# Three matrix products into a bank that is overwritten, ahead of each of the first 22 steps of a two-layer feed-forward

## The chip, the cores and the metric

The kernel runs on one core of one Trainium2 chip. The metric is the device time of one execution in microseconds (us); lower is better. The core has a matrix engine (TensorE: PE, with PEld for its weight loads), a vector engine (VectorE: DVE), a scalar engine (ScalarE: ACT), GpSimd (POOL) and SyncE (SP), whose queue issues the transfers from memory. Each engine runs its own list of instructions in order and waits on semaphores for the others. The matrix engine's clock is throttled: the profile shows at each time what was granted, 1.0 (2.4 GHz) or 0.5 (1.2 GHz).

## The reference

Three stages follow each other. Attention with gates runs over 768 time steps, for 2 batches of 8 heads of width 40; then come a feed-forward with a sigmoid gate, and a normalised feed-forward with a SiLU gate, each over 1536 tokens of width 320 with 1536 hidden units.

```python
for t in range(S):                                   # attention, S = 768
    m_new = np.maximum(f_gate[:, :, t] + m, i_gate[:, :, t])
    f_stab = np.exp(f_gate[:, :, t] + m - m_new)
    i_stab = np.exp(i_gate[:, :, t] - m_new)
    C = f_stab[..., None, None] * C + i_stab[..., None, None] * np.einsum('bhd,bhe->bhde', vt, kt)
    n = f_stab[..., None] * n + i_stab[..., None] * kt
    h_tilde = np.einsum('bhde,bhe->bhd', C, qt)
    y[:, :, t] = o * h_tilde / np.maximum(np.abs(nq), 1.0)
...
gate = 1.0 / (1.0 + np.exp(-(x @ w_gate)))           # first feed-forward
x = gate * (x @ w_val) @ w_out
...
xn = x / rms * rms_g                                 # second feed-forward
g = xn @ w_gate
out = g * (1.0 / (1.0 + np.exp(-g))) * (xn @ w_val) @ w_out
```

## The kernel before

**Attention** is cut into 6 chunks of 128 time steps, each for both batches. A chunk is a string of small jobs (`a_f`, `a_s`, `a_p`, `a_inter`, `a_pv`, `a_u`, `a_h`, `a_x`): the matrix engine multiplies queries and keys (`a_s`, L323), VectorE weights the result (`a_p`, L332, after a scan in `a_f`, L306), the matrix engine multiplies by the values (`a_pv`, L391), VectorE adds the carried state and divides (`a_h`, L417 to L429), and `a_x` transposes the chunk (L467 to L470) into `xT`, the input of the first feed-forward, of which ScalarE writes the high half (L446 to L453) and VectorE the low one (`sub`, L194).

**The first feed-forward** is 6 chunks times 12 slices of 128 hidden units, 72 steps. A step (`moe`) is 16 products of 256 columns (L689) into a PSUM bank with the tag `g`, then a sigmoid on ScalarE (L691), a product on VectorE (L692), and a split into two halves `h` (L694 and a `sub` on GpSimd). Two steps later `moe_out` multiplies `h` by the slice of the output weights (L727, 6 products of 320 columns). There are two banks `g`, so the products of a step wait until VectorE has read the bank of the step before last.

The first 24 steps are interleaved by `ORDER = '000000111100001100111111'`, a digit for the chunk: steps 0 to 5 are slices 0 to 5 of chunk 0, steps 6 to 9 are slices 0 to 3 of chunk 1, and so on. In that stretch the weights of the layer arrive: each slice is loaded (L139), its 8-byte numbers are converted on ScalarE and VectorE (`conv_w`, L161 to L191) and split into two halves (`split_w`, L194 to L207). Attention on chunk 1 has to be done before step 6. The second feed-forward (`moe2`, L703, products of 512 columns, and L752) follows after the 72 steps, and its weights are loaded and converted over the last of them.

**The order.** The code lists jobs by step numbers (`at`, `ev`); then the framework's scheduler puts the instructions of each engine into an order, with a model of its own for their durations, and every engine keeps that order on the chip.

**Unread products** exist in the program already. `bank(tag)` hands out a PSUM bank, and if a number stands on the list `pend`, it takes it off and first issues so many products of the tile `warm` into that bank (L86, L87). The first real product overwrites them. Before, `pend` is filled twice, with 13 at the very start (L591) and with 1 later (L622). `warm` is then a zeroed tile of a pool that is closed at L675.

Of the kernel before, what the change touches and what calls it, by code (L numbers as in the profile page):

```python
# [9 lines left out]
BF16 = mybir.dt.bfloat16  # L10
# [19 lines left out]
GR = 80  # L30
SKEW = 2
WARM = 13
KEEP = (2, 14)
C2S = (8, 10)
XF = (0, 0, 0, 0, 0, 0, 0, 0, 0, 0, 0, 0)
# [29 lines left out]
def mlstm_moe_kernel(ctx, tc, gate_if, gate_s, qk, qg, tok, w1, w2, rms_g, cst, out):  # L65
# [15 lines left out]
    def bank(tag):  # L81
        if tag in cycle:
            turn[tag] += 1
            tag = cycle[tag][turn[tag] % len(cycle[tag])]
        t = (ps_2 if tag in "ag" else ps_1).tile([128, 512], F32, tag=tag, name=tag)
        for _ in range(pend.pop() if pend else 0):  # L86
            nc.tensor.matmul(out=t, lhsT=warm[:, 0:128], rhs=warm, start=True, stop=True)  # L87
        return t

    pend = []  # L90

    def keep(t, i, c, n):

        if c == 0 and i % 2 == 0:
            w = min(512 - i * n, 64 * KEEP[n == L])
            if w > 0:
# [11 lines left out]
    ident4 = const.tile([128, 4, L], F32, name="ident4")  # L108
# [84 lines left out]
    def sub(eng, out, a, b):  # L193
        eng.tensor_tensor(out=out, in0=a, in1=b, op=ALU.subtract)  # L194
# [340 lines left out]
    pos = {k: i for i, k in enumerate(seq)}  # L535
# [33 lines left out]
    for f in range(NF):  # L569
        t = pos[1, 0, f]  # L570
# [5 lines left out]
        t = W2A + int(W2B * f)  # L576
# [8 lines left out]
    warm = gp.tile([128, 512], BF16, name="warm")  # L585
# [4 lines left out]
    nc.scalar.activation(out=er[:, 0:1], in_=mhalf[0:GR], func=AF.Exp)  # L590
    pend.append(WARM)  # L591
    bank("o0")
# [81 lines left out]
    gates_r4()  # L674
    stk.close()  # L675
    hp = pool("hp", 3)
    more.append(pool("xn", 2))
    xn, xg = [], []
    load_qk(1, 0)
# [3 lines left out]
    def moe(c, f):  # L683
        x = xT[1, c]
        w = wg_t[f]
        g = bank("g").rearrange("p (m t) -> p m t", m=2)
        for m in range(2):
            for i, (ws, xs) in enumerate(ORD):
                nc.tensor.matmul(out=g[:, m, :], lhsT=w[:, m, ws, :], rhs=x[xs // 3][:, xs % 3, :], start=(i == 0), stop=(i == 7))  # L689
        sg = p2.tile([128, T], F32, tag="sig", name="sig")  # L690
        nc.scalar.activation(out=sg, in_=g[:, 0, :], func=AF.Sigmoid, scale=2.0 ** -8)  # L691
        nc.vector.tensor_tensor(out=sg, in0=sg, in1=g[:, 1, :], op=ALU.mult)  # L692
        h = hst[1, c, f] = hp.tile([128, 2, T], F32R, tag="h", name="h")
        nc.scalar.activation(out=h[:, 0, :], in_=sg, func=AF.Copy)  # L694
        sub(nc.gpsimd, h[:, 1, :], sg, h[:, 0, :])
# [73 lines left out]
    for i in range(min(ev), len(seq) + SKEW):  # L769
# [6 lines left out]
        if 0 <= i < len(seq):  # L776
            layer, c, f = seq[i]
            wo_t_used[layer, f] = wo_t[f]
            (moe if layer == 1 else moe2)(c, f)
        while 0 <= i and done < len(seq) and done <= i - (SKEW if seq[done][0] == 1 else 1):  # L780
            layer, c, f = seq[done]
# [86 lines left out]
```

## Time and profile before

| what | value |
|---|---|
| median of three runs | 525.17 us (522.12 to 525.74) |
| the profiled execution | 525.99 us, span 523.9 us |
| matrix engine busy | 492.4 us, 94% of the span |
| VectorE, ScalarE, GpSimd busy | 316.0, 249.6, 234.6 us |
| mean granted clock of the matrix engine | 0.944 |

The span is what the profile covers; 2.1 us lie around it. The shares are means over stages of different kinds: until about 113 us the weights of the first layer and the first attention chunks are prepared, from there to 250 us the matrix engine runs through the first layer, and then the weights of the second layer are made ready beside it.

### The profile page before, as it was taken

To read this page: it belongs to the slowest core of one execution; us is meant where nothing else is said; L and a number is where in the kernel's file an instruction comes from. 1 tells how busy PE (TensorE), PEld (TensorE's weight loads), DVE (VectorE), ACT (ScalarE), POOL (GpSimd) and SP (SyncE) were. 2 spreads that over 40 slices of the span, in tenths; PEclk is the share of its full clock that TensorE was granted. 3 is DMA by queue.
4 is the path that set the end of the run, shared out by engine and by line. 5 is a ranking of instruction groups with operands and counts; after the bars stand their busy time and mean duration, and the time that the engine had idled before them with its cause. 6 is when DMAs were issued, how large, how long until landed. Compare 5 with 4: busy or idle time off the path is not lost.

```text
span 523.9 us, 8522 instructions
## 1 busy us (share of the span) xinstructions
PE 492.4 (94%) x3248; PEld 450.9 (86%) x3248; DVE 316.0 (60%) x581; ACT 249.6 (48%) x535; POOL 234.6 (45%) x265
## 2 busy tenths in 40 slices
PE   6969866999999999999999888999999999999997
PEld 3859855989999999999999877788888888888886
DVE  5796898994535958758678998742343223432223
ACT  5586949762633454445558874632243222431222
POOL 1584794474253746535235997542112121122220
PEclk9575696989999999999999999999999999999999
DMA  6938545711220322202245422200000000000001
GB/s 211 317 112 294 176 145 198 244 47 35 85 74 1 81 84 74 79 2 90 77 157 210 144 94 76 76 1 1 1 35 17 0 1 0 27 24 1 1 1 50
DMA packets 13342, 43.79 MB, mean 84 GB/s; under 512 B 1846, under 2 KB 5158, under 8 KB 13302
## 3 DMA queue, kind: packets, MB, share of 16 engines
q1 hardware_dynamic: 13158, 43.12, 25.0%
q8 instruction: 25, 0.41, 0.3%
q10 hardware_dynamic: 144, 0.14, 0.1%
q14 instruction: 15, 0.12, 0.1%
HBM read 41.21 MB, written 2.01 MB: 82 GB/s over the span
## 4 chain that ended last, share of the span: by engine, by line
PE 62%; DVE 9%; ACT 6%; DMA 4%; issue 3%; POOL 2%; POOLq 0%; DVEq 0%; SPq 0%; ACTq 0%
PE g L689 13%; PE a L703 11%; PE o L752 11%; PE g L703 11%; PE o L727 7%; DMA wraw<-in_w_dram 4%; PE o L689 3%; DVE wg L194 1%; POOL wg L194 1%; DVE wc L184 1%; ACT wraw L161 1%; DVE wc L191 1%; ACT wraw L165 1%; PE a L323 1%; ACT wraw L164 1%
## 5 line engine op out<-in xcount | busy, mean ns | idle before, releaser
L689 PE MATMUL g<-xT,wg 128*128 128x256 f32 x896 | 134.1, 300 | 4.1 <-ACT wg L201 1.8
L689 PEld LDWEIGHTS g<-xT,wg 128*128 128x128 f32 x896 | 122.9, 204 | 6.2 <-DVE sig L692 2.7
L194 POOL TENSOR_TENSOR h<-sig,h 128x256 fp32r<-128x256 f32 x72 | 65.4, 911 | 91.7 <-ACT h L694 90.2
L194 POOL TENSOR_TENSOR ft<-p,fb 128x512 fp32r<-128x512 f32 x35 | 45.5, 1303 | 133.7 <-ACT fb L712 133.7
L727 PE MATMUL o<-wo,h 128*128 128x320 f32 x432 | 81.8, 320 | 7.4 <-POOL h L194 4.0
L706 DVE TENSOR_TENSOR p<-p,g 128x512 f32<-128x512 f32 x36 | 24.6, 687 | 90.1 <-ACT p L705 90.1
L727 PEld LDWEIGHTS o<-wo,h 128*128 128x128 f32 x432 | 66.8, 194 | 11.1 <-POOL h L194 6.8
L752 PE MATMUL o<-wo,fb 128*128 128x320 f32 x288 | 53.1, 311 | 0.0
L703 PE MATMUL g<-xT,wg 128*128 128x512 f32 x180 | 50.8, 394 | 0.1
L712 ACT ACTIVATE fb<-p 128x512 fp32r<-128x512 f32 (+1 forms) x37 | 22.8, 619 | 58.7 <-DVE p L711 52.4
L705 ACT ACTIVATE p<-g 128x512 f32<-128x512 f32 x36 | 21.3, 596 | 60.6 <-PE g L703 56.2
L752 PEld LDWEIGHTS o<-wo,fb 128*128 128x128 f32 x288 | 45.9, 188 | 2.4 <-ACT fb L712 0.2
L703 PE MATMUL a<-xT,wg 128*128 128x512 f32 x180 | 47.8, 390 | 0.0
L694 ACT ACTIVATE h<-sig 128x256 fp32r<-128x256 f32 x72 | 29.6, 414 | 37.2 <-DVE sig L692 35.2
L703 PEld LDWEIGHTS a<-xT,wg 128*128 128x128 f32 x180 | 33.5, 188 | 6.8
L703 PEld LDWEIGHTS g<-xT,wg 128*128 128x128 f32 x180 | 32.5, 188 | 5.6 <-ACT xT L446 0.4
L711 DVE TENSOR_TENSOR p<-p,a 128x512 f32<-128x512 f32 (+1 forms) x37 | 24.6, 672 | 21.0 <-PE a L703 20.3
L689 PE MATMUL o<-xT,wg 128*128 128x256 f32 x256 | 35.1, 285 | 0.4 <-DVE sig L692 0.4
L161 ACT ACTIVATE wraw<-wraw 128x960 f32<-128x960 f32 x24 | 26.3, 1097 | 19.3 <-DMA wraw<-in_w_dram 19.3
L692 DVE TENSOR_TENSOR sig<-sig,g 128x256 f32<-128x256 f32 x56 | 23.0, 413 | 20.1 <-ACT sig L691 18.6
L194 POOL TENSOR_TENSOR wg<-wc,wg 128x256 fp32r<-128x256 f32 (+1 forms) x34 | 27.1, 810 | 15.0 <-ACT wg L201 12.2
L689 PEld LDWEIGHTS o<-xT,wg 128*128 128x128 f32 x256 | 32.6, 191 | 0.9 <-DVE sig L692 0.9
(224 smaller groups left out, 873.1 us busy)
## 6 DMA issues: line engine op xcount, KB each, us to landing
wraw<-in_w_dram SPq DMA_DIRECT2D x24, 960.0 KB
tok<-in_tok_dram SPq DMA_DIRECT2D x12, 488.0 KB
fb<-fd SPq DMA_DIRECT2D x20, 256.0 KB
raw<-in_qk_dram SPq DMA_DIRECT2D x24, 160.0 KB
out_dram<-xn SPq DMA_DIRECT2D x12, 160.0 KB
qg<-in_qg_dram SPq DMA_DIRECT2D x10, 180.0 KB
rmsg<-in_rms_g_dram SPq DMA_DIRECT2D x1, 160.0 KB
cs<-in_cst_dram ACTq DMA_DIRECT2D x1, 136.5 KB
```

Of the source, the lines that this page charges most:

```text
L161: nc.scalar.activation(out=hi.bitcast(F32), in_=hi.bitcast(F32), func=AF.Copy, scale=2.0 ** -111)
L194: eng.tensor_tensor(out=out, in0=a, in1=b, op=ALU.subtract)
L689: nc.tensor.matmul(out=g[:, m, :], lhsT=w[:, m, ws, :], rhs=x[xs // 3][:, xs % 3, :], start=(i == 0), stop=(i == 7))
L692: nc.vector.tensor_tensor(out=sg, in0=sg, in1=g[:, 1, :], op=ALU.mult)
L694: nc.scalar.activation(out=h[:, 0, :], in_=sg, func=AF.Copy)
L703: nc.tensor.matmul(out=g[m], lhsT=w[:, m, ws, :], rhs=x[xs // 3][:, xs % 3, :], start=(i == 0), stop=(i == 7))
L705: nc.scalar.activation(out=sg, in_=g[0], func=AF.Sigmoid, scale=2.0 ** -8)
L706: nc.vector.tensor_tensor(out=sg, in0=sg, in1=g[0], op=ALU.mult)
L711: nc.vector.tensor_tensor(out=sg[:, n], in0=sg[:, n], in1=g[1][:, n], op=ALU.mult)
L712: nc.scalar.activation(out=h[0][:, n], in_=sg[:, n], func=AF.Copy)
L727: nc.tensor.matmul(out=o, lhsT=h[:, hs, n], rhs=w[:, ws, :], start=(f == 0 and i == 0), stop=(f == NF - 1 and i == 2))
L752: nc.tensor.matmul(out=o, lhsT=h[hs][:, n], rhs=w[:, ws, :], start=(f == 0 and i == 0), stop=(f == NF - 1 and i == 2))
```

## The change

`BUSY = (22, 3)`: in each of the first 22 steps of the first feed-forward, `moe` puts a 3 on `pend` before it takes its bank `g`. So three products of 512 columns go into that bank ahead of the step's 16, 66 in all. Since the zeroed tile is gone by then, `warm` becomes a view of the identity tile `ident4`, read as 16-bit numbers.

```diff
@@ -30,6 +30,7 @@
 GR = 80
 SKEW = 2
 WARM = 13
+BUSY = (22, 3)
 KEEP = (2, 14)
@@ -674,6 +675,7 @@
     gates_r4()
     stk.close()
     hp = pool("hp", 3)
+    warm = ident4.rearrange("p u t -> p (u t)").bitcast(BF16)[:, 0:512]
     more.append(pool("xn", 2))
@@ -683,6 +685,8 @@
     def moe(c, f):
         x = xT[1, c]
         w = wg_t[f]
+        if pos[1, c, f] < BUSY[0]:
+            pend.append(BUSY[1])
         g = bank("g").rearrange("p (m t) -> p m t", m=2)
```

The scheduler sees 66 more products, and orders other work differently as well. Line numbers of the changed kernel are 1 higher up to L677 and 4 higher from L689 on; its L88 is L87 of before.

**The matrix engine at steps 0 and 1.** The start of the first feed-forward, before:

```order
L400 MATMUL o_345<-vv,kk 80x84
L280 MATMUL a<-cs,gr 128x80
L689 MATMUL g<-xT,wg 128x256 x7
L280 MATMUL a<-cs,er 128x80
L689 MATMUL g<-xT,wg 128x256 x9
L283 MATMUL a<-el,selg 120x30
```

and in the change:

```order
L401 MATMUL o_345<-vv,kk 80x84
L88 LDWEIGHTS ident_80
L88 MATMUL g<-ident_80 128x512
...
L281 MATMUL a<-cs,gr 128x80
L693 MATMUL g<-xT,wg 128x256 x7
L281 MATMUL a<-cs,er 128x80
L693 MATMUL g<-xT,wg 128x256 x9
```

Six unread products, those of step 0 and of step 1, stand ahead of step 0 and of the transposes of the gates.

**The matrix engine at steps 6 to 9**, where chunk 1 enters. Before:

```order
L467 MATMUL a<-cs,x 128x128
L468 MATMUL a<-cs,x 128x128
L323 MATMUL a<-raw 128x128 x4
L470 MATMUL a<-cs,rem 128x128
L727 MATMUL o_632<-wo,h 128x320 x2
...
L689 MATMUL g<-xT,wg 128x256 x32
L369 MATMUL a<-cm,qg 128x126 x2
L369 MATMUL a<-cm,qg 128x84
L391 MATMUL a<-vv,p 128x42 x8
L689 MATMUL g<-xT,wg 128x256 x16
```

and in the change:

```order
L471 MATMUL a<-cs,rem 128x128
L324 MATMUL a<-raw 128x128 x4
L88 LDWEIGHTS ident_80
L88 MATMUL g<-ident_80 128x512
...
L693 MATMUL g<-xT,wg 128x256 x10
L324 MATMUL a<-raw 128x128 x4
L693 MATMUL g<-xT,wg 128x256 x22
L392 MATMUL a<-vv,p 128x42 x8
L88 LDWEIGHTS ident_80
L88 MATMUL g<-ident_80 128x512
...
L693 MATMUL g<-xT,wg 128x256 x16
```

The three products of step 7 stand among the transposes and output products ahead of step 6; those of step 6 stand further up, ahead of the transposes L467. From step 8 on the three stand right ahead of their step.

**VectorE, at the end of attention on chunk 1**, before (`x`, L429, is what the transposes wait for):

```order
L407 SCALAR_TENSOR_TENSOR C_106<-C_106,gb,a 120x126 x2
L407 SCALAR_TENSOR_TENSOR C_106<-C_106,gb,a 80x84
L427 SCALAR_TENSOR_TENSOR r<-hs,r 128x8
L194 TENSOR_TENSOR wg<-wc,wg 64x128
L194 TENSOR_TENSOR wo<-wc,wo 128x320
L428 RECIPROCAL r<-r 128x8
L182 TENSOR_SCALAR wc<-wraw 128x960
L429 TENSOR_TENSOR x<-x,r 128x320
```

and in the change:

```order
L195 TENSOR_TENSOR wo<-wc,wo 128x320
L429 RECIPROCAL r<-r 128x8
L430 TENSOR_TENSOR x<-x,r 128x320
L183 TENSOR_SCALAR wc<-wraw 128x960
L408 SCALAR_TENSOR_TENSOR C_106<-C_106,gb,a 120x126 x2
L408 SCALAR_TENSOR_TENSOR C_106<-C_106,gb,a 80x84
```

The update of the state (L407) and a shift of weights (L182) moved behind `x`. Further on, a scan of the next chunk (L306) moved from ahead of the low half of `xT` to behind it.

## Rows read from the trace of the kernel before

**Rows 1.** The page's slices, 40 of 13.1 us each: busy tenths, clock granted.

```profile
PE   6969866999999999999999888999999999999997
DVE  5796898994535958758678998742343223432223
PEclk9575696989999999999999999999999999999999
```

**Rows 2.** Busy time by stretch: PE, PEld, DVE, ACT, POOL; clock; DMA.

```profile
27.00:89.00 62.00, 46.45 (x249) 41.67 (x249) 52.34 (x70) 46.02 (x77) 42.52 (x49) 0.72 0.53 179
89.00:149.00 60.00, 59.28 (x442) 57.62 (x442) 44.13 (x84) 33.31 (x74) 31.75 (x43) 0.94 0.38 119
149.00:209.00 60.00, 60.00 (x538) 59.02 (x537) 38.22 (x94) 25.56 (x69) 30.96 (x40) 1.00 0.19 53
...
280.00:340.00 60.00, 54.58 (x348) 48.56 (x347) 54.10 (x81) 42.98 (x107) 47.05 (x48) 1.00 0.33 114
```

**Rows 3.** Waits of PE, 27 to 89 us: total us, times, longest.

```profile
PE a L467 <- DVE x L429: 4.2, 1, 4.2
...
PE g L689 <- ACT wg L201: 1.8, 1, 1.8
```

**Rows 4.** Waits of PE, 89 to 149 us: all there are.

```profile
PE o L727 <- POOL h L194: 0.6, 1, 0.6
PE g L689 <- DVE sig L692: 0.2, 1, 0.2
```

**Rows 5.** The chain that ended last, 108 to 122 us: start, us, what.

```profile
110.75 2.35 DVE wc L184
...
113.49 3.66 PE g L689 x16
...
118.45 1.95 PE g L689 x16
```

**Rows 6.** Timeline of PE, 57 to 95 us: start, us; idle before in brackets.

```profile
57.88 3.57 PE L689 MATMUL g<-xT,wg 128*128 128x256 f32 x15
...
77.04 0.46 PE L727 MATMUL o<-wo,h 128*128 128x320 f32 x2
81.67 0.30 PE L467 MATMUL a<-cs,x 128*128 128x128 f32 x1 [4.18 <-DVE x L429]
...
83.99 0.48 PE L470 MATMUL a<-cs,rem 128*128 128x128 f32 x1 [0.54 <-ACT rem L465]
85.25 1.43 PE L727 MATMUL o<-wo,h 128*128 128x320 f32 x4 [0.78 <-ACT h L694]
...
89.31 5.61 PE L689 MATMUL g<-xT,wg 128*128 128x256 f32 x32
```

**Rows 7.** Busy time by stretches of one clock, columns as in Rows 2.

```profile
62.30:82.70 20.40, 12.89 (x97) 11.53 (x97) 20.06 (x29) 12.85 (x22) 17.73 (x20) 1.00 0.47 168
82.80:92.90 10.10, 8.79 (x36) 7.64 (x35) 8.93 (x13) 9.09 (x21) 5.55 (x8) 0.50 0.66 196
...
113.50:116.80 3.30, 3.30 (x15) 3.30 (x16) 2.87 (x5) 2.57 (x7) 1.75 (x3) 0.50 0.33 100
```

**Rows 8.** Products of 512 columns: chain, second layer; busy time of L87 alone.

```profile
421.70 1.81 PE a L703 x8
...
4.24:5.50 1.26, 1.26 (x7) 0.49 (x5) 1.00 0.94 381
```

**Rows 9.** Timeline of DVE, 78 to 92 us.

```profile
78.01 0.80 DVE L407 SCALAR_TENSOR_TENSOR C<-C,gb,a 120x126 f32<-120x126 f32 x3
...
80.42 0.70 DVE L182 TENSOR_SCALAR wc<-wraw 128x960 int32<-128x960 int32 x1
...
86.94 1.21 DVE L306 TENSOR_TENSOR_SCAN ft<-fb,ident 128x512 f32<-128x512 f32 x1
...
89.61 1.51 DVE L194 TENSOR_TENSOR xT<-a,xT 128x256 fp32r<-128x256 f32 x5
```

**Rows 10.** The chain that ended last, 249 to 256 us: first load for layer two.

```profile
252.53 0.10 ACT sig L691
252.63 6.28 DMA wraw<-in_w_dram
```

## The prediction

> **What bounds the kernel now.** I read the slices first, to see where the matrix engine is idle and where its clock is low [rows 1]. Both lie in the first nine slices, up to about 117 us; from there to 250 us every slice is full and at full clock. So the 22 steps fall into a part with idle time and a part without, and the question is where the border runs.
>
> Busy time by stretch draws it [rows 2]. From 27 to 89 us, where steps 0 to 5 run and attention on chunk 1 ends, the matrix engine is busy for 46.45 of 62 us, so 15.5 us are idle. From 89 to 149 us, where steps 6 to 21 run, it is busy for 59.28 of 60 us, and from 149 to 209 us for all 60.
>
> The waits say what the idle time is. Before 89 us, the longest is for `x`, the last vector operation of attention on chunk 1, 4.2 us; another 1.8 us is for the weights of slice 3 [rows 3]. Between 89 and 149 us only two waits are left, 0.6 and 0.2 us [rows 4].
>
> The chain of waits needs care. Up to 113.49 us it runs over weight conversions on VectorE and ScalarE, and only then goes to the matrix engine [rows 5]. It could be read so that the matrix engine has room until 113 us. But it has been working without a pause of note since step 6 at 89.31 us [rows 6, 4]: two engines are full side by side there, and whatever is put in front of the fuller one comes out at the end.
>
> **What a product costs.** A product of 512 columns in a dense run at full clock takes 1.81 us / 8 = 0.226 us in the second layer [rows 8]. The products of `warm` at the very start are the same form as the added ones: 7 touch a stretch of 1.26 us, about 6 whole ones, 0.21 us each [rows 8]. Between 0.21 and 0.226 I take 0.226, since it comes from a full count, amid weight loads and other work as here. At half clock 15 products of 256 columns take 3.57 us [rows 6], 0.238 each, so about 0.45 for 512 columns at the most. Their weight loads ran beside the products at the start too (0.49 us of PEld in 1.26 us), and I cost them at nothing; the product before each covers them.
>
> The Trainium skill (TensorE: Matmul & The Clock Gate, Back-to-back issue gap) gives about 131 ns for a product of 512 columns in a stream of weight loads and products. By that the 42 products below would be 5.5 us, an estimate, and the sum +2.4 us; the row of 0.226 us disagrees, and I follow the row.
>
> **The change part by part.**
>
> *Steps 0 to 7: 24 products, taken at nothing.* At half clock they need 24 x 0.45 = 10.8 us, at full clock 5.4 us, against 15.5 us idle [rows 2]. Idle time has to lie in the right place, so piece by piece: the six at the front delay step 0, but ScalarE and VectorE are at weights then, and the matrix engine waits later anyway, with 1.8 us for slice 3 among it [rows 3]. Those of steps 4 to 6 fall between 62 and 82 us, where the engine is idle for 7.5 us of 20.4 while VectorE is busy for 20.06 [rows 7]. What hides them is VectorE. If that cover went, the engine would pay up to 10.8 us.
>
> *The start of steps 6 and 7: -0.7 us.* The scheduler moved three vector operations out of the way: the state update (0.80 us) and a shift (0.70 us) from ahead of `x`, and a scan (1.21 us) from ahead of the low half of `xT` [rows 9]. If all comes through, steps 6 and 7 end 2.7 us sooner. On the other side, six products at half clock (2.7 us) stand in the way of step 6, with gaps of 0.54 and 0.78 us to fall into [rows 6]; that is 1.4 us later. Between -2.7 and +1.4 I take the middle, -0.7: the vector rows say sooner, but from 85.25 us on the matrix engine worked without a pause before too, so it can't follow entirely.
>
> *Steps 8 to 21: 14 x 3 = 42 products x 0.226 = +9.5 us.* They stand directly ahead of their step, in a list that has no gaps. They use the bank `g` of that step, so where a step would wait for its bank, they wait too, and hide nothing. The real products behind them are late by 0.68 us a step; sigmoid, VectorE and GpSimd are late with them, but have time to spare there (VectorE 44.1 us busy of 60 [rows 2]).
>
> *What is given back: -0.8 us* for the two waits after 89 us [rows 4], since the vector engine no longer makes a later matrix engine wait; *and -1.6 us for the clock.* Step 12 runs at half clock from 113.5 to 116.8 us [rows 7], with 16 products in 3.66 us, against 1.95 us for step 13 at full clock [rows 5]. The pause ahead of it is one of the waits that go. I take 1.6 of the 1.7 us, with bounds of 0 and 1.7.
>
> *After step 21: nothing.* The first load of the second layer's weights starts at 252.63 us, when a sigmoid of the first layer has ended [rows 10], so it moves along with the steps. The 5.4 us idle between 280 and 340 us [rows 2] are waits for those weights, which become late by the same amount; they hide nothing.
>
> **Sum:** 9.5 - 0.8 - 1.6 - 0.7 = **+6.4 us**, so 532.4 us against the execution's own 525.99 us. That execution lies 0.8 us above the median of the runs shown and just above the highest. I take off half of that: **532.0 us**, 1.3% above the median. With the bounds of the terms (0.7 us less by the cheaper product, 2.0 us each way at step 6, 1.6 us more by the clock) the forecast's own range is 529.5 to 534.5.
>
> **The rivals.**
>
> *A. The matrix engine has room until 113 us.* Then only steps 12 to 21 pay: 30 x 0.226 = 6.8, less 0.8, 1.6 and 0.7, which is +3.7 us, or 529.3 us. For it speaks the chain, which lies on VectorE and ScalarE up to step 12 [rows 5]; against it the 59.28 us of 60 [rows 2]. It is in part true if steps 6 and 7 end sooner. Chance 0.19.
>
> *B. Nothing is given back.* The clock falls around step 6 as before and again later, and the products ahead of step 6 are paid at half speed: 9.5 - 0.8 + 1.4 = +10.1 us, or 535.7 us. For it speaks that the engine was busy for 8.79 of 10.1 us at half clock around step 6 [rows 7], so being busy alone didn't bring the clock back at once. Chance 0.14.
>
> *C. Not slower: the products keep the clock up, and the work behind them closes the gap ahead of step 6.* The place is the stretch from 77.5 us, where step 5's work ends, to 89.31 us [rows 6], the price up to 11.8 us. All of it gained would be -11.8 + 9.5 - 0.8 - 1.6 = -4.7 us, or 520.9 us; it decides from the point where step 6 starts before 82.2 us, which is 7.1 us sooner. Against it: the matrix engine waits there for VectorE, which is full and not on that clock [rows 7, 3]. Chance 0.05.
>
> The Trainium skill (TensorE: Matmul & The Clock Gate, Why this matters for your kernels) advises keeping the engine continuously busy to hold the full clock, which is the rule behind C. By it the clock would stay up around step 6; the trace has half clock there after the idle 4.2 us, which agrees, but the rule doesn't say that the faster engine ends anything sooner.
>
> *D. The products are much cheaper than the row,* near 0.13 us, as on the page above: 9.5 becomes 5.5 and the sum +2.4 us, 528.0 us. Both groups of rows for 512 columns speak against it. Chance 0.02.
>
> **How the numbers follow.** The forecast has 0.60, A 0.19, B 0.14, C 0.05, D 0.02. For 8 times in 10 I go from 528.0 to 536.0 us, which takes in the forecast, B's value and most of A, and leaves out C and the tails. One per cent of the median, about what a measurement of this kernel can tell from no change, is 5.25 us, so the border lies at 530.4 us. Three quarters of the forecast's range and B lie above it: 0.45 + 0.14 = 0.59 slower. The rest of the forecast, A and D are within: 0.15 + 0.19 + 0.02 = 0.36. C is 0.05 faster.
>
> **What would show each step right or wrong.** In the profile of the changed kernel: step 6 should start within 3 us of 89.3 us, and idle time of the matrix engine before it should have shrunk by the length of 24 products; a start before 82.2 us means C. From step 8 on, a step with its output products should take 0.68 us more than now, with no waits between 89 and 155 us; if steps 8 to 11 take more but step 12 starts where it did, A was right. The clock should be 1.0 from step 8 on; a stretch at 0.5 behind it means B. The first load of the second layer should come some 6 us later, and the rest of the trace be shifted by the same. The prediction is wrong if the order on VectorE, which the scheduler also changed, makes weights or attention late somewhere that these rows don't show, or if that later stretch takes up the delay.

## The result, and the profile after

| | before | changed |
|---|---|---|
| median (nine runs each) | 523.29 us (522.12 to 525.74) | 528.29 us (527.18 to 533.05) |
| the profiled execution | 525.99 us, span 523.9 us | 527.76 us, span 525.7 us |

The change makes the kernel slower: 1.0108 times before, 95% interval 1.0074 to 1.0143, which is 3.9 to 7.5 us; the medians differ by 5.0 us. The forecast was 532.0 us, between 528.0 and 536.0. The changed kernel's nine times lie in two groups, six from 527.2 to 528.9 us and three from 531.6 to 533.1. The two profiles come from opposite ends, that of before from above all its nine times and that of the change from its lower group, so they differ by only 1.8 us. Disturbed executions are left out of all ratios; one of the thirteen profiles, that of the kernel without products in the order of that with 24, is of one (545.1 us), and only times up to 44 us, ahead of all the steps compared here, are taken from it.

The slices of the changed kernel, of 13.1 us each, answer to [rows 1]:

```profile
PE   6969798989999999999999888999999999999997
DVE  6786999973544858659578999752343223432223
PEclk9575979999999999999999999999999999999999
```

The matrix engine is fuller in slices 6 and 7 and a little emptier in slice 9, and the clock is whole from slice 7 on, where before it dipped in slices 7 and 9. Its busy time by stretch, columns as in [rows 2]:

```profile
27.00:89.00 62.00, 52.05 (x297) 45.44 (x296) 54.34 (x76) 47.82 (x77) 47.00 (x49) 0.78 0.59 201
89.00:149.00 60.00, 57.33 (x437) 51.74 (x436) 37.01 (x69) 28.20 (x66) 29.46 (x37) 1.00 0.23 75
149.00:209.00 60.00, 60.00 (x537) 58.71 (x536) 41.34 (x97) 26.39 (x69) 32.25 (x42) 1.00 0.26 74
```

Up to 89 us it is busy 5.6 us more. From 89 to 149 us it is not fuller but emptier, 57.33 against 59.28 us, and the waits of that stretch (to 155 us; against [rows 4]) say why:

```profile
PE o L731 <- POOL h L195: 2.1, 1, 2.1
PE g L88 <- DVE sig L696: 0.5, 1, 0.5
```

The two waits that I had going away, 0.8 us, are 2.6 us now. The timeline of the matrix engine (start, us; idle before in brackets; against [rows 6]) shows where the lead came from and where that wait stands:

```profile
65.94 3.21 PE L392 MATMUL a<-vv,p 128*128 128x42 f32 x14 [2.17 <-DVE C L408]
...
77.61 0.33 PE L468 MATMUL a<-cs,x 128*128 128x128 f32 x1 [0.51 <-DVE x L430]
...
79.98 0.82 PE L88 MATMUL g<-ident 128*128 128x512 bf16 x3
...
83.80 1.35 PE L693 MATMUL g<-xT,wg 128*128 128x256 f32 x10
85.08 1.16 PE L324 MATMUL a<-raw 40*128 40x128 f32 x8
86.17 2.90 PE L693 MATMUL g<-xT,wg 128*128 128x256 f32 x22
...
92.45 2.26 PE L693 MATMUL g<-xT,wg 128*128 128x256 f32 x16
...
108.20 0.85 PE L731 MATMUL o<-wo,h 128*128 128x320 f32 x4 [2.12 <-POOL h L195]
108.89 0.82 PE L88 MATMUL g<-ident 128*128 128x512 bf16 x3
109.36 2.27 PE L693 MATMUL g<-xT,wg 128*128 128x256 f32 x16
```

The transposes of `x` start 4.06 us sooner than before, and the 4.18 us of waiting for them are 0.51. Step 6 starts at 83.80 us instead of 89.31, and its 32 products take 1.35 + 2.90 = 4.25 us instead of 5.61. Step 12 takes 2.27 us instead of 3.66. The clock of two stretches ahead of step 6 (columns as above):

```profile
66.00:72.60 6.60, 6.60 (x28) 5.76 (x29) 6.54 (x7) 2.11 (x6) 6.44 (x7) 0.50 0.49 171
73.00:83.00 10.00, 7.89 (x51) 5.86 (x49) 9.07 (x18) 9.94 (x17) 6.87 (x9) 1.00 0.34 106
```

Half clock comes earlier now, behind the 2.17 us of waiting for the state update (`C`) at 64 us, and in this profile no stretch of it is left after 73 us. Last, the chain that ended last, 108 to 122 us (start, us, what; against [rows 5]), has the price of the added products:

```profile
108.20 0.85 PE o L731 x4
109.05 0.66 PE g L88 x3
109.71 1.91 PE g L693 x16
...
113.60 0.75 PE g L88 x3
114.35 1.91 PE g L693 x16
...
117.82 0.66 PE g L88 x3
```

Three take 0.66 us, 0.22 each. Step by step the lead is used up:

| start of step | before | changed | difference |
|---|---|---|---|
| 6 | 89.31 | 83.80 | -5.5 |
| 8 | 97.13 | 92.45 | -4.7 |
| 12 | 113.49 | 109.36 | -4.1 |
| 14 | 121.12 | 118.13 | -3.0 |
| 24 | 154.53 | 156.53 | +2.0 |
| end of the span | 523.9 | 525.7 | +1.8 |

So in these two profiles the change costs 7.5 us from step 6 to step 24, and before step 6 it gains 5.5 that the forecast had as 0.7. The experiments ask which part of the change does which.

### The profile page after: what moved, and what is told of

Same layout as the page of the kernel before. It is cut to its first block, busy times and chain, and to the rows that moved or that the text cites. A ratio compares the mean times of both kernels' runs of the same rounds, so it can differ in the third digit from the quotient of the medians.

```text
span 525.7 us, 8646 instructions
## 1 busy us (share of the span) xinstructions
PE 499.8 (95%) x3314; PEld 451.3 (86%) x3314; DVE 316.2 (60%) x581; ACT 249.4 (47%) x535; POOL 241.7 (46%) x265
## 4 chain that ended last, share of the span: by engine, by line
PE 60%; DVE 11%; ACT 8%; DMA 6%; issue 3%; POOL 2%; SPq 0%; POOLq 0%
PE g L693 11%; PE o L756 11%; PE g L707 11%; PE a L707 11%; PE o L731 7%; DMA wraw<-in_w_dram 6%; PE o L693 3%; ACT wraw L162 2%; DVE wg L195 2%; PE g L88 1%; POOL wg L195 1%; PE a L324 1%; DVE wc L185 1%; DVE wc L192 1%; ACT wg L202 1%
## 5 line engine op out<-in xcount | busy, mean ns | idle before, releaser
L693 PE MATMUL g<-xT,wg 128*128 128x256 f32 x896 | 130.4, 295 | 2.9 <-DVE sig L696 1.6
L693 PEld LDWEIGHTS g<-xT,wg 128*128 128x128 f32 x896 | 118.9, 196 | 7.1 <-DVE sig L696 2.3
L195 POOL TENSOR_TENSOR h<-sig,h 128x256 fp32r<-128x256 f32 x72 | 66.5, 925 | 85.4 <-ACT h L698 84.7
L731 PE MATMUL o<-wo,h 128*128 128x320 f32 x432 | 80.2, 315 | 6.5 <-POOL h L195 5.4
L731 PEld LDWEIGHTS o<-wo,h 128*128 128x128 f32 x432 | 65.4, 190 | 9.9 <-POOL h L195 8.0
L707 PEld LDWEIGHTS g<-xT,wg 128*128 128x128 f32 x180 | 32.5, 188 | 5.7 <-ACT xT L447 0.4
L695 ACT ACTIVATE sig<-g 128x256 f32<-128x256 f32 x56 | 21.4, 382 | 25.9 <-PE g L693 21.2
```

Of the source, the lines that this page charges most:

```text
L707: nc.tensor.matmul(out=g[m], lhsT=w[:, m, ws, :], rhs=x[xs // 3][:, xs % 3, :], start=(i == 0), stop=(i == 7))
L731: nc.tensor.matmul(out=o, lhsT=h[:, hs, n], rhs=w[:, ws, :], start=(f == 0 and i == 0), stop=(f == NF - 1 and i == 2))
```

## The experiments

They come in two kinds: fewer products, with the scheduler left alone, and the order pinned, so that products and order can be told apart.

**Products in steps 0 to 7 only** (24 products), the first of three variants of one line, all compared on one chip:

```diff
-        if pos[1, c, f] < BUSY[0]:
+        if pos[1, c, f] < 8:
```

> Only steps 0 to 7 get their three products (24 in all); VectorE has the order of the changed kernel up to step 8. My theory: these 24 lie in waits or bring the start of step 6 forward, and cost nothing: -3 to 0 us against the kernel before, step 6 starting at 82 to 88 us. The rival that every added product is paid: +5.3 us (24 x 0.22).

Measured: 522.41 us, 0.9969 times before (0.9947 to 0.9991). The 24 products cost nothing, and step 6 starts at 86.12 us, 3.2 sooner.

**Products in steps 8 to 21 only** (42 products).

```diff
-        if pos[1, c, f] < BUSY[0]:
+        if 8 <= pos[1, c, f] < BUSY[0]:
```

> Only steps 8 to 21 get three products (42 in all); the order on VectorE is that of the kernel before until step 8. My theory: all 42 are paid, 42 x 0.22 = +9.2 us, less the 0.8 us of waits and 1.6 us of half clock at step 12: +6.8 us against the kernel before, more than the whole change costs, since the gain of the first steps is missing. The rival that the matrix engine has room until step 12: 30 x 0.22 - 2.4 = +4.2 us.

Measured: 530.14 us, 1.0130 (1.0103 to 1.0158), which is +6.8 us. Step 6 starts at 88.96 us, as before, and step 12 runs at full clock. The forecast's sum without the start of steps 6 and 7 is 9.5 - 0.8 - 1.6 = +7.1.

**Products in steps 12 to 21 only** (30 products).

```diff
-        if pos[1, c, f] < BUSY[0]:
+        if 12 <= pos[1, c, f] < BUSY[0]:
```

> Only steps 12 to 21 get three products (30 in all). My theory: 30 x 0.22 = +6.6 us, less up to 2.4 us of waits and half clock: +4.2 to +6.6 us, and 2.6 us less than with the products of steps 8 to 11 as well. The rival that the matrix engine has room until step 12: the same time as with the products of steps 8 to 21, within 1 us.

Measured: 529.69 us, 1.0118 (1.0090 to 1.0146). Twelve products fewer save 0.5 us, not 2.6. That is nearer to rival A, that steps 8 to 11 are free; but the two kernels also differ in order (the multiplications of queries and keys of `a_s` stand ahead of step 12 in one and behind it in the other) and in waits (0.95 us left in this one, 0.4 in the other), so it took a run with the order held.

**The kernel before again**, as a control, with a profile of its own.

> The kernel before, unchanged, as a control: 0 within 1 us of itself. Its new profile tells how far the start of step 6 (89.31 us in the first one) and the stretches at half clock move between executions: if step 6 starts 3 us or more sooner here, the sooner start seen with the change is no work of the change; if it stays within 1.5 us of 89.3, it is.

Measured: 523.94 us, 1.0001 (0.9980 to 1.0022). Step 6 starts at 89.95 us, and step 12 is again at half clock. So neither the early step 6 nor the full clock at step 12 is chance.

**The order held.** In the next five kernels each engine's instructions, SyncE's transfers among them, are tied in the order that another kernel's had on the chip. The ties set no semaphore, and unread products are left out of them. `PLACES`, a packed list, says whose order it is:

```diff
+        n0 = len(nc.cur_bb.bb.instructions)
...
+        unread.update(k.name for k in nc.cur_bb.bb.instructions[n0:])
...
+    own = [k for k in nc.cur_bb.bb.instructions[base:] if k.name not in unread]
+    for places in json.loads(zlib.decompress(base64.b85decode(PLACES))).values():
+        for p, q in zip(places, places[1:]):
+            tc.add_manual_dep(own[q], own[p].name, mybir.DependencyInfo(mybir.DependencyClass.NoSync, mybir.DependencyReason.DATA), reason="order")
```

**No products, in the order of the kernel with 24.** The kernel before with the ties above; `PLACES` from the kernel with products in steps 0 to 7. Against that one, the edit on the products is

```diff
-        if pos[1, c, f] < 8:
-            pend.append(BUSY[1])
```

> The kernel before with no added product at all, but every engine keeps the order of the run in which steps 0 to 7 have theirs. Theory order (the scheduler's order brings step 6 forward, mostly the weight load moved ahead of other loads on SP's queue and VectorE's jobs moved behind x): step 6 starts at 86 us within 1.5, and the time is that of the run with the 24 products within 1 us, -1.6 us against the kernel before. Theory clock (the 24 products keep TensorE's clock up, and that brings step 6 forward): step 6 starts at 89 to 90 us, and the time is that of the kernel before, 0 within 1 us.

Measured: 521.50 us, 0.9949 (0.9931 to 0.9968). Without a single added product this order alone beats before by 0.5%, and by the two ratios it is 1.6% below the changed kernel. It was the fastest kernel run.

**24 products, in the order of before.** The ties, with `PLACES` from the kernel before, and against the changed kernel

```diff
-        if pos[1, c, f] < BUSY[0]:
+        if pos[1, c, f] < 8:
```

> The 24 products of steps 0 to 7, with every other instruction in the order of the kernel before on all engines. Theory order: nothing gets sooner, step 6 at 89 to 91 us, time 0 to +1.5 us. Theory clock: step 6 at 86 us, -1.6 us, half clock gone from 54 to 62 us. If every product were paid: +5.3 us.

Measured: 523.15 us, 0.9978 (0.9957 to 0.9998). Timeline of its matrix engine:

```profile
81.83 0.45 PE L473 MATMUL a<-cs,x 128*128 128x128 f32 x1 [3.75 <-DVE x L435]
...
88.63 4.00 PE L699 MATMUL g<-xT,wg 128*128 128x256 f32 x32
```

The wait for `x` is still 3.75 us, and step 6 starts 0.7 us sooner: with the order of before the products hardly move it. What differs is the clock: the 32 products of steps 6 and 7 take 4.00 us instead of 5.61, and step 12 runs at full clock. The engine is then sooner at the steps behind, and waits more there, 1.8 us from 89 to 155 us instead of 0.8:

```profile
PE o L737 <- POOL h L200: 1.0, 2, 0.6
PE g L699 <- DVE sig L702: 0.8, 2, 0.6
```

**No products, in the order of the changed kernel.** The ties, with `PLACES` from the changed kernel, and against it

```diff
-        if pos[1, c, f] < BUSY[0]:
-            pend.append(BUSY[1])
```

> The kernel before with no added product, every engine in the order of the changed kernel. Theory order, with 42 x 0.22 us paid behind step 8: 6 to 8 us less than the changed kernel, so -1 to -3 us against the kernel before, with step 6 at 84 to 86 us. Theory clock: 0 within 1 us, since the order alone brings nothing.

Measured: 525.61 us in the median, ratio 1.0006 (0.9981 to 1.0032), with times in two groups, 521.5 to 524.0 and 525.4 to 526.1 us; the -1 to -3 us that I expected did not come. The profile is of the fastest, 521.49 us. Step 6 starts at 85.61 us, 3.7 sooner than before, so the order does that. It also brings the longer wait after 89 us (waits of the matrix engine, 89 to 155 us):

```profile
PE o L733 <- POOL h L199: 3.0, 1, 3.0
PE g L695 <- DVE sig L698: 0.7, 1, 0.7
```

**66 products, in the order of before.** The changed kernel with the ties, `PLACES` from the kernel before, and its own line as it was:

```diff
         if pos[1, c, f] < BUSY[0]:
             pend.append(BUSY[1])
```

> All 66 products, every other instruction in the order of the kernel before. Theory order: step 6 at 89 to 91 us, +6.4 to +8.5 us against the kernel before, more than the changed kernel. Theory clock: like the changed kernel, +5 us within 1 us.

Measured: 531.96 us, 1.0146 (1.0118 to 1.0173), or +7.6 us; step 6 starts at 90.18 us, and between 89 and 155 us no wait of the matrix engine is left.

**36 products (steps 0 to 11), in the order of before.** The ties, with `PLACES` from the kernel before, and against the changed kernel

```diff
-        if pos[1, c, f] < BUSY[0]:
-            pend.append(BUSY[1])
+        if 0 <= pos[1, c, f] < 12:
+            pend.append(3)
```

> 36 products, those of steps 0 to 11, every other instruction in the order of the kernel before. It lies between the run with the 24 products of steps 0 to 7 (0.9978 of the kernel before) and the one with all 66 (1.0146) in the same order, 8.8 us apart. My theory, each product behind step 8 is paid: the 12 of steps 8 to 11 cost 2.6 us less at most 0.8 us of waits, so +0.6 to +1.5 us against the kernel before. Rival A, the matrix engine has room until step 12: as with 24 products, -1.1 us, within 0.6.

Measured: 523.75 us, 1.0009 (0.9991 to 1.0028). In one order, then, 24, 36 and 66 products give 0.9978, 1.0009 and 1.0146. The +0.5 us is just below what I expected for paid products, and 1.6 above rival A's. The 12 of steps 8 to 11 cost 0.31%, 1.6 us, of 2.6 us of product time. The two intervals overlap, so this difference is likely and not sure. In the profiles it is smaller: from the start of step 6 to that of step 12 it takes 24.19 us with 24 products and 25.10 with 36, 0.9 us more. Of the 1.8 us of waits it has 0.6 left (from 89 to 155 us), so 1.2 us of the products lie in them, and where the other 0.5 us went is not shown:

```profile
PE g L91 <- DVE sig L702: 0.6, 2, 0.4
```

The 30 behind them cost 1.37%, 7.2 us, against 30 x 0.22 = 6.6. In the profiles the stretch from the start of step 12 to that of step 24 is 6.1 us longer with 66 products than with 36. The one from step 6 to step 12 is 1.8 us longer too, though both kernels have the same products there: the 32 products of steps 6 and 7 took 6.19 us, mostly at half clock, in the one and 4.00 in the other.

**The changed kernel once more**, for its second group of times.

> The changed kernel once more, for a second profile. Its nine times so far lie in two groups, 527.2 to 528.9 and 531.6 to 533.1 us. If this one falls into the upper group, its steps should show where the 4 us arise: by theory order, in the steps up to 12 where loads and vector work set the pace; by theory clock, in a stretch at half clock that the first profile doesn't have.

Measured: 532.0 us, from the upper group. The difference arises ahead of step 1. Waits of SyncE's queue in the first 60 us (total us, times, longest), first the changed kernel's first profile, then this one:

```profile
SPq L296 <- DMA fd<-gr: 3.8, 1, 3.8
```

```profile
SPq L296 <- DMA fd<-gr: 6.4, 1, 6.4
```

The queue waits for the gates' store to memory before it reads them back, 2.6 us longer here; the store was also issued 1.1 us later. The scan on VectorE that needs them (timeline), in the first profile and in this one:

```profile
29.60 1.23 DVE L307 TENSOR_TENSOR_SCAN ft<-fb,ident 128x512 f32<-128x512 f32 x1 [1.22 <-DMA fb<-fd]
```

```profile
32.85 1.23 DVE L307 TENSOR_TENSOR_SCAN ft<-fb,ident 128x512 f32<-128x512 f32 x1 [3.51 <-DMA fb<-fd]
```

It is 3.25 us late, the weight load of slice 3 leaves the queue 3.24 us late, and step 6 starts 3.4 us later, step 24 4.3, the end of the span 4.1. Between steps 6 and 24 the other 0.9 us arises: the 32 products of steps 6 and 7, which took 4.25 us in the first profile, take 6.33 here (timeline), since the granted clock is 0.50 from 88 to 94 us in spite of the products ahead:

```profile
87.20 2.11 PE L693 MATMUL g<-xT,wg 128*128 128x256 f32 x10
...
91.25 4.22 PE L693 MATMUL g<-xT,wg 128*128 128x256 f32 x22
```

So a late landing at 30 us, ahead of all that waits in the queue, goes with the upper group here. It doesn't decide alone: with 24 products in free order that wait was 5.9 us, and the execution took 520.75 us.

**The order of the changed kernel without products, once more.**

> The changed kernel's order without products once more, for a second profile. Its times lie at 521.5 to 524.0 and at 525.4 to 526.1 us; the profiled one was the lowest. If this one falls into the upper group, the place of the 4 us should show in its steps, and be the same as in the changed kernel's.

Measured: 524.61 us. Up to step 12 it is level with its first profile (110.50 and 110.38 us). Then the two part, by the clock. Busy time of this one from 108 to 114.8 us, and of its first profile:

```profile
108.00:114.80 6.80, 5.54 (x24) 5.54 (x25) 3.19 (x6) 2.68 (x7) 3.42 (x5) 0.50 0.00 0
```

```profile
108.00:114.80 6.80, 5.11 (x45) 4.80 (x46) 4.21 (x7) 2.99 (x8) 4.58 (x6) 1.00 0.00 0
```

The same wait of 3.0 us stands ahead in both, and the engine came back at half clock in one only. Step 13 starts at 116.38 us instead of 114.35. None of the eight profiles of kernels with products has that dip at step 12; both of the kernel before have it. Since the first profile here has no dip without any product, the products go with the full clock at step 12 and are not shown to be needed for it.

## Why the prediction was right, and which step was not

**The time: inside the range, and near its lower end.** The 528.29 us lie 0.3 us above the lower end of 528.0 to 536.0 and outside the forecast's own 529.5 to 534.5. By the border as written, 530.4 us, it is on the side of no change, which had 0.36 against 0.59 for slower. As a ratio, 1.0108, it is just past the one per cent that the border stood for, and the interval lies across it.

Of the 3.7 us between 532.0 and 528.3, 2.3 are the starting point: I began at 525.6, and the median of nine runs before is 523.3. The other 1.4 are the sum, +6.4 against +5.0. That the sum came so near is in part luck: the first profile of the changed kernel is only 1.8 us above that of before, since the start of step 6 was mis-sized by 4.8 us, and the second, in which a late landing and half clock took that back, 6.0. Of the signs that I named, the clock of 1.0 from step 8 on came true in both profiles. The start of step 6 within 3 us of 89.3 failed in the first, at 83.80, and 2.6 us of waits after 89 us were left where I had expected none.

**The price per product: right.** 0.22 us against the 0.226 that I took from the second layer. (My 0.45 us at half clock is a little low: twice the 0.238 of its row is 0.48, so 24 products would need 11.4 us and not 10.8. Nothing else hangs on it.) By the 131 ns of the Trainium skill (TensorE: Matmul & The Clock Gate, Back-to-back issue gap) the 42 would have been 5.5 us, an estimate; the row decided, and no run shows that figure.

**Steps 0 to 7 at nothing: right.** With the order of before, 24 products gave 0.9978. In their own order they gave 0.9969 where that order without them gave 0.9949; that would be 1.0 us, but the intervals overlap.

**Steps 8 to 21 with the waits and the clock: right in the sum, 7.1 us forecast.** From the start of step 6 to that of step 24 it was 65.2 us before, 72.7 in the change (+7.5) and 72.5 with the order of before (+7.3). In the latter the terms can be followed: 42 x 0.22 = 9.2, less 0.8 for the waits, which are gone, less 1.7 for the clock at step 12, and 0.6 more for step 6, which ran at half clock there too:

```profile
90.18 6.19 PE L699 MATMUL g<-xT,wg 128*128 128x256 f32 x32
```

That row is the timeline of the kernel with 66 products in the order of before; the terms give +7.3. In the changed kernel the same sum is made otherwise. The waits are 1.8 us longer, not 0.8 shorter, since the engine comes to steps 8 to 11 some 4 us sooner while GpSimd and VectorE do not; and step 6 at full clock gives 1.4 us back. 9.2 + 1.8 - 1.7 - 1.4 is +7.9, against 7.5. In its second profile the stretch took 73.6 us, +8.4: waits of 0.8 us are left there, as many as before, and steps 6 and 7 took 6.33 us instead of 5.61, so 9.2 - 1.7 + 0.7 is +8.2. So the clock around step 6 is a term that I had left to rival B and not put into the sum. The profiles show it at either level in either order: with 24 and 36 products in the order of before it was whole there, with 66 it was not.

**The start of steps 6 and 7, -0.7 us: mis-sized, the step that failed.** It was -5.5 us in the profile and outside my bounds of -2.7 to +1.4 (in the second profile, -2.1, it was inside them). The runs split it in two. What ScalarE waits for at 45 us, the weights of slice 3, is the point that separates them:

| | slice 3 on ScalarE, to before | step 6, to before | from the one to the other |
|---|---|---|---|
| changed kernel | -3.2 | -5.5 | -2.3 |
| changed kernel again | +0.2 | -2.1 | -2.3 |
| its order, no products (two profiles) | -1.7, -2.3 | -3.7, -4.3 | -2.0, -2.0 |
| 24 products, free order | -1.2 | -3.2 | -2.0 |
| order of before, 24, 36, 66 products | +0.3, +0.1, +0.8 | -0.7, -0.4, +0.9 | -1.0, -0.5, +0.1 |
| before again | +0.6 | +0.6 | 0.1 |

From slice 3 on, every kernel in the new order gains 2.0 to 2.3 us. That fits the reordered vector operations, which I had bounded at 2.7 and then cut to a middle value on account of the six products in the way; they did not stand in the way, and in the order of before the gain is 1.0 at most. The rest, up to 3.2 us, is there already at 45 us, and my working did not look at that place. The likely cause lies in SyncE's queue. Its timeline before, then in the change:

```profile
36.80 0.36 SPq L124 DMA_DIRECT2D raw<-in_qk_dram  x1
37.43 0.33 SPq L139 DMA_DIRECT2D wraw<-in_w_dram  x1
37.81 0.36 SPq L124 DMA_DIRECT2D raw<-in_qk_dram  x1
```

```profile
36.68 0.42 SPq L140 DMA_DIRECT2D wraw<-in_w_dram  x1
37.20 0.69 SPq L125 DMA_DIRECT2D raw<-in_qk_dram  x2
37.94 0.46 SPq L140 DMA_DIRECT2D wraw<-in_w_dram  x1
```

The weights of slice 3 now leave ahead of the queries and keys. ScalarE's first use of them, before and in the change:

```profile
45.76 1.09 ACT L161 ACTIVATE wraw<-wraw 128x960 f32<-128x960 f32 x1 [5.06 <-DMA wraw<-in_w_dram]
```

```profile
42.55 1.11 ACT L162 ACTIVATE wraw<-wraw 128x960 f32<-128x960 f32 x1 [3.06 <-DMA wraw<-in_w_dram]
```

From issue to use 8.3 us have become 5.9. The other profiles agree: it is 5.3 to 6.0 us in the six of the two new orders, 7.7 to 8.6 in the seven where one load of queries and keys still stands ahead. So about 2.5 us go with the place in the queue. The other 0.8 us are an earlier issue, and that is likely chance: it hangs on when the gates' store lands, and the 5.5 us from that store's issue to the first read-back behind it are the shortest of all thirteen profiles. In the changed kernel's other profile it took 7.8 us, and the whole 3.2 us were lost. I had read the order of the matrix engine and of VectorE, and not that of the queue.

**What of this reaches the end.** With 66 products the new order gives 1.0108 where the old gives 1.0146, 2 us less, with intervals that overlap; without products the order of the changed kernel gives 1.0006, and that of 24 products 0.9949. So a start 3.7 to 5.5 us sooner is worth between nothing and 2.7 us: part goes into the wait for `h` (3.0 us against 0.6), part into half clock behind that wait.

**After step 21 nothing: right.** Step 24 is 2.0 us late and the span 1.8; with the order of before 8.2 and 7.3, in the changed kernel's second profile 6.3 and 5.9. But the first load of the second layer was not the one of [rows 10]. SyncE's queue begins with them at 242.97 us before and at 244.99 in the change (timelines, `x5` and `x4` loads):

```profile
242.97 31.30 SPq L139 DMA_DIRECT2D wraw<-in_w_dram  x5
```

```profile
244.99 21.61 SPq L140 DMA_DIRECT2D wraw<-in_w_dram  x4
```

That is 2.0 us later, the same as step 24. The chain only shows the load on which it runs.

**The rivals.** A (steps 8 to 11 free) gives nearly the measured time, and is true in part: with the order held these steps cost 0.9 us by the profiles and 1.6 by the ratios, of 2.6. The room for most of the rest is not the 0.8 us of waits of before, but the 1.8 us that open up when step 6 runs at full clock. The changed kernel comes out near A's 529.3 us above all because its order starts step 6 sooner. With the order free, 12 products did cost only 0.5 us, and how much of that was the scheduler and how much the waits is not separated. B (nothing given back) is out: step 12 is at full clock. Its first half can come true: with 66 products in the order of before, and in the second profile of the changed kernel, step 6 was at half clock again. C (the clock closes the gap ahead of step 6) is out: with 24 products in the order of before the gap was 3.75 us. D is out by 0.66 us for three.

**Open.** Why the order of the changed kernel alone ends level with before while that of 24 products gains 0.5%: the half clock at step 12 accounts for 2 us between its two profiles, but the slower group (525.4 to 526.1 us) has no profile. Nor was the one weight load moved in the queue alone, so its 2.5 us are read from the profiles and not shown by a run of their own.

## What to carry to other kernels

Products that are put in to keep an engine busy are free only where it waits; where its list is full each costs its whole duration, and one row of a like product prices it to a few per cent. Work that is added under a scheduler also gets a new order on every engine and on the DMA queue: compare the order at the first late load, not only at the place of the change, and test order and work apart. Such an order can be worth a good part of the change, here 0.5% gained without any of the added work, against 1.1% lost by the change as a whole.

## What the runs showed that I had not expected

A matrix engine busy without a gap is not always granted its full clock. Busy time of the kernel before, from 40 to 50 us:

```profile
40.00:50.00 10.00, 10.00 (x46) 9.55 (x45) 6.40 (x8) 4.89 (x5) 5.83 (x7) 0.50 1.02 339
```

It was busy for all 10 us and stayed at 0.50, level 1.2 GHz, while in the changed kernel the stretch from 73 to 83 us was at 1.00 with 7.89 of 10 us busy. And one small store, that of the gates, took 5.5 to 8.0 us over the thirteen profiles from its issue to the first read-back that waited for it; the queue stood still for it between 2.2 and 6.4 us, and two profiles of one kernel with 2.6 us between those waits ended 4 us apart.
